# Attention and two feed-forward layers on one core: a third place for raw weights, weight sums at other points of the program, and operand splits in earlier slots

## The chip, the core and the metric

The kernel runs on one core of a Trainium2 chip. A core has five engines that run their own instruction streams side by side: TensorE (PE in the profile, with its weight loads as PEld), VectorE (DVE), ScalarE (ACT), GpSimd (POOL) and SyncE (SP, which here only issues DMA transfers). They wait for each other through semaphores, and each engine executes its stream strictly in order: an instruction that waits holds up everything behind it on its engine. Matrix products go from SBUF through TensorE into PSUM; DMA brings data from HBM into SBUF. The metric is the device time of one execution in microseconds (us), median of several runs.

## The reference

Attention with a soft cap, then a gated layer (SiLU), then a second two-layer network with a parametric ReLU. All of it is float32.

```python
batch, n_heads, seq, head_dim = (2, 12, 448, 64)       # attention
n_tokens, d_model, d_ff = (896, 768, 1536)             # first network; the second has d_ff 2048

scores = scale * np.matmul(q, k.transpose(0, 1, 3, 2))
scores = cap * np.tanh(scores / cap)
attn = np.exp(scores - max); attn = attn / (attn.sum(-1) + 1e-09)
x = attn @ v                                            # heads joined: 896 x 768

xn = x / sqrt(mean(x * x) + 1e-06) * rms_g
g = xn @ w_gate;  x = (silu(g) * (xn @ w_val)) @ w_out

h = x @ w_in;  out = (max(h, 0) + alpha * min(h, 0)) @ w_out2
```

## The kernel before

**Products.** A float32 operand is split into a high part (type fp32r) and a low remainder; a product is high x high + high x low + low x high. ScalarE writes the high part (a cast), VectorE the remainder (original minus high part).

**Weights.** The weights lie in HBM as 68 units of 128 x 768. A unit goes through `w_load` (a DMA of 768 KB issued by SP into a place tagged `raw`, two of them), `w_top` (a cast on ScalarE, L103), `w_bits` (VectorE, L107, which writes the float32 tile `wt` and frees the place), `w_hi` (ScalarE, L120, tile `wh`) and `w_lo` (VectorE, L124, tile `wl`). `w_next(u)`, called right after `w_bits(u)`, issues the load two units further on in `conv_seq`.

**Attention.** 12 pairs of heads with 4 steps each (48 steps). A step holds `qk` (TensorE, scores), `soft` (tanh and exp on ScalarE) and, two steps later, `pv` (TensorE). The list `later` says which other work is written behind which step: `prep` splits the next pair's inputs on VectorE, `evac` copies a pair's result out of PSUM and sends its row sums to a tile `gt` by DMA, `recip` (VectorE) turns these into reciprocals `th`/`tl` and spreads them by two DMAs into `r2` (on GpSimd's queue, the last ones on SP's), `norm` multiplies on TensorE (`rps`, L286) and VectorE (L288, L289), squares on GpSimd (ScalarE for the last four pairs) and adds up `s2` on GpSimd. `rms` (TensorE L309, ScalarE's square root L311, VectorE's reciprocal L312) gives `rstd` of one of the two batches; `xnorm` (L325) applies it.

**The two long layers** ("g", the gate and value weights, and "z", `w_in`) use Strassen's scheme with seven products P1 to P7 per group of two weight blocks (6 groups in g, 4 in z). They need four units (A11, A21, A22, A12) and four sums of them, made on GpSimd (L115): S1 = A21 + A22, S2 = S1 - A11 (written over A11), S3 = A11 - A21 (over A21), S4 = A12 - S2 (over A12). The activations have operands B11, B21, B22, T1 to T4, each with a high and a low tile.

**The two short layers** ("o", `w_out`, and "f", the last `w_out`) read the results of a long layer as moving operands. `ksplit` splits one block of eight rows of them (three casts on ScalarE, L727), `ksplit_low` makes the three remainders on VectorE (L494), in the tiles that the operands T1 to T4 and B11 to B22 leave free. `oslot` computes three outputs at a time, each in a PSUM tile of its own.

**Order.** After the attention the program is a list of 94 slots (one Strassen product of 18 matmuls, or a step of o or f of 36). `do(n, rank, fn, ...)` hangs work on slot n; it is written behind the slot's matmuls, by rank: 0 for `w_hi` (of slot n + 2) and `w_top`, 1 for work on results (`silu`, `times`, `prelu_a` on ScalarE, `prelu_b` and the additions `add21`, `add22`, `u2` on VectorE), 2 for `w_lo` and `ksplit_low`, 3 for `bits`, 4 for the sums, 5 for operands and `ksplit`. g starts at slot 0, o at 38, z at 50, f at 78. PSUM holds four pair tiles in turn: two `s`, two `m`; a product that takes a tile waits until the work on its last content is done.

The functions that the change touches follow.

## Time and profile before

| | us |
|---|---|
| median of 3 runs (644.24 to 651.46) | 648.99 |
| the profiled execution | 650.39 |
| its span from the first to the last instruction | 648.6 |
| TensorE busy (93% of the span) | 602.7 |
| VectorE busy (63%) | 407.8 |
| ScalarE busy (55%) | 354.3 |
| GpSimd busy (19%) | 121.0 |
| time on the chain that ended last: TensorE 66%, VectorE 9%, ScalarE 4%, DMA 4% | |

A row of a timeline or of a wait list names the engine, the line of the kernel, and out<-in by the program's tile names. `L343` are the Strassen products, `L568`, `L570`, `L572` the three kinds of matmul of o and f. TensorE's clock has two levels, 2.4 GHz (a granted clock of 1.00) and 1.2 GHz (0.50); its mean over the span is 0.97.

### The profile page before, as it was taken

How to read it: one execution, taken by the hardware profiler on the slowest of the kernel's cores; microseconds unless marked ns; L12 is line 12 of the kernel's file. 1: busy time of each engine (PE TensorE's matmuls, PEld its weight loads, DVE VectorE, ACT ScalarE, POOL GpSimd, SP SyncE). 2: the span in 40 equal slices, each digit the busy share in tenths (PEclk: the TensorE clock that was granted, in tenths of full speed). 3: DMA queues.
4: the chain of work that ended last, by engine and by line, in shares of the span. 5: the costliest groups of instructions: out<-in, count | busy, mean ns of one | idle time of the engine just before them, and what ended most of it. 6: DMA issues, size and time to landing. Idle time of an engine off the chain costs nothing.

```text
span 648.6 us, 6899 instructions
## 1 busy us (share of the span) xinstructions
PE 602.7 (93%) x2672; PEld 511.0 (79%) x2672; DVE 407.8 (63%) x439; ACT 354.3 (55%) x435; POOL 121.0 (19%) x71
## 2 busy tenths in 40 slices
PE   5999989797999999996999999989789769999997
PEld 4666655475998999995999999979679669999996
DVE  7456679848998966866553565867786567533200
ACT  6999988634734554436444444646566648434101
POOL 0012542253014441310000052301351000000000
PEclk9999999997999999999899999989989969999999
DMA  8556642110033444123224652003321421264002
GB/s 303 197 189 244 231 149 87 28 64 36 0 114 130 146 147 147 49 74 122 99 97 147 199 190 98 0 1 132 112 98 50 146 98 49 98 220 157 1 1 85
DMA packets 18632, 73.47 MB, mean 113 GB/s; under 512 B 5672, under 2 KB 6056, under 8 KB 18600
## 3 DMA queue, kind: packets, MB, share of 16 engines
q1 hardware_dynamic: 15592, 72.82, 32.0%
q0 software_dynamic: 2864, 0.21, 0.4%
q8 instruction: 21, 0.34, 0.2%
q14 instruction: 11, 0.09, 0.0%
q10 hardware_dynamic: 144, 0.00, 0.0%
HBM read 70.14 MB, written 2.75 MB: 112 GB/s over the span
## 4 chain that ended last, share of the span: by engine, by line
PE 66%; DVE 9%; ACT 4%; DMA 4%; issue 2%; POOL 0%; SPq 0%; ACTq 0%; DVEq 0%; POOLq 0%
PE s L343 17%; PE m L343 14%; PE s L570 6%; PE s L572 6%; PE s L568 6%; PE m L570 5%; PE m L572 5%; PE m L568 5%; DMA raw<-w_in 3%; DVE wl L124 1%; DVE b L494 1%; DVE rstd L312 1%; ACT top L103 1%; ACT ks L727 1%; DVE b L794 1%
## 5 line engine op out<-in xcount | busy, mean ns | idle before, releaser
L124 DVE TENSOR_TENSOR wl<-wt,wh 128x768 fp32r<-128x768 f32 x98 | 110.3, 1131 | 89.9 <-ACT wh L120 89.6
L103 ACT CAST top<-raw 128x768 f16<-128x768 bf16 x68 | 73.1, 1076 | 126.2 <-DMA raw<-w_in 125.2
L115 POOL TENSOR_TENSOR wt<-wt 128x768 f32<-128x768 f32 x40 | 89.0, 2229 | 276.9 <-DVE wt L107 198.7
L120 ACT CAST wh<-wt 128x768 fp32r<-128x768 f32 x98 | 80.8, 832 | 68.8 <-PE s L570 15.4
L107 DVE SCALAR_TENSOR_TENSOR wt<-raw,top 128x768 uint32<-128x768 uint32 x68 | 68.3, 1006 | 17.0 <-ACT top L103 12.2
L343 PE MATMUL s<-xh,wh 128*128 128x448 f32 x234 | 62.1, 374 | 2.3 <-DVE b L794 2.3
L343 PE MATMUL s<-xh,wl 128*128 128x448 f32 x234 | 61.5, 371 | 0.0
L343 PE MATMUL s<-xl,wh 128*128 128x448 f32 x234 | 61.4, 370 | 0.0
L343 PE MATMUL m<-xh,wh 128*128 128x448 f32 x186 | 50.9, 380 | 10.2 <-ACT b L447 6.0
L199 PE MATMUL s<-hi 128*128 128x448 f32 x96 | 48.5, 506 | 6.8 <-DVE hi L375 6.5
L568 PE MATMUL s<-ks,wh 128*128 128x448 f32 x176 | 51.0, 371 | 3.9 <-ACT ks L727 3.9
L572 PE MATMUL s<-ks,wl 128*128 128x448 f32 x176 | 50.9, 371 | 0.0
L343 PE MATMUL m<-xh,wl 128*128 128x448 f32 x186 | 49.5, 375 | 1.2 <-DVE wl L124 1.2
L343 PEld LDWEIGHTS s<-xh,wh 128*128 128x128 f32 x234 | 44.2, 190 | 7.8 <-issue 3.2
L343 PE MATMUL m<-xl,wh 128*128 128x448 f32 x186 | 49.2, 373 | 0.0
L343 PEld LDWEIGHTS m<-xh,wh 128*128 128x128 f32 x186 | 35.8, 194 | 15.6 <-ACT b L447 6.4
L343 PEld LDWEIGHTS s<-xh,wl 128*128 128x128 f32 x234 | 44.3, 190 | 4.6 <-DVE wl L124 0.2
L343 PEld LDWEIGHTS s<-xl,wh 128*128 128x128 f32 x234 | 44.4, 190 | 4.4
L568 PE MATMUL m<-ks,wh 128*128 128x448 f32 x160 | 46.6, 373 | 0.5 <-ACT ks L727 0.5
L572 PE MATMUL m<-ks,wl 128*128 128x448 f32 x160 | 46.8, 374 | 0.0
L209 ACT ACTIVATE pt<-s,cinv 128x896 f32<-128x896 f32 (+1 forms) x48 | 43.6, 909 | 5.8 <-PE s L199 4.1
L210 ACT ACTIVATE pt<-pt,cap_t 128x896 f32<-128x896 f32 (+1 forms) x48 | 45.6, 950 | 1.6
(118 smaller groups left out, 987.1 us busy)
## 6 DMA issues: line engine op xcount, KB each, us to landing
raw<-w_in SPq DMA_DIRECT2D x68, 768.0 KB, 4.4
rw<-qk_in SPq DMA_DIRECT2D x11, 928.0 KB, 4.9
vt<-v_in SPq DMA_DIRECT2D x12, 416.0 KB, 5.5
out<-o SPq DMA_DIRECT2D x5, 448.0 KB, 2.5
rw<-qk_in SPq DMA_DIRECT2D x1, 480.0 KB, 4.4
rw<-qk_in SPq DMA_DIRECT2D x1, 448.0 KB, 5.4
out<-o SPq DMA_DIRECT2D x2, 224.0 KB, 2.0
gt<-ea SPq DMA_DIRECT2D x12, 1.8 KB, 1.6
```

Source lines behind the costliest of these rows:

```text
L103: nc.scalar.copy(top_of[u].bitcast(F16)[:, 1::2], raw_t[u].bitcast(BF16)[:, 4:4 * UW + 4:4])
L107: nc.vector.scalar_tensor_tensor(out=f_t[u].bitcast(U32), in0=raw_t.pop(u).bitcast(U32)[:, 1:2 * UW + 1:2], scalar=13, in1=top_of.pop(u), ...
L115: nc.gpsimd.tensor_tensor(out=t, in0=f_t[a], in1=f_t[b], op=op)
L120: nc.scalar.copy(h_t[u], f_t[u].rearrange("p (k m) -> p k m", m=P))
L124: nc.vector.tensor_tensor(out=l_t[u], in0=f_t[u].rearrange("p (k m) -> p k m", m=P), in1=h_t[u], op=ALU.subtract)
L199: nc.tensor.matmul(s[:, n, :S], hi[i][:, S + o:S + o + P], t[hd], start=(m == 0), stop=(m == len(mm) - 1),)
L209: nc.scalar.activation(out=t[:, :n], in_=s[:, :n, :S], func=AF.Tanh, scale=cinv)
L210: nc.scalar.activation(out=t[:, :n], in_=t[:, :n], func=AF.Exp, scale=cap_t)
L343: nc.tensor.matmul(ps[:, r, :S], lhs, rhs, start=first and n == 0, stop=n == len(mm) - 1, skip_group_check=True,)
L568: nc.tensor.matmul(dst[l], wh[:, o, :], xh[l], start=first, stop=False)
L570: nc.tensor.matmul(dst[l], wh[:, o, :], xl[l], start=False, stop=False)
L572: nc.tensor.matmul(dst[l], wl[:, o, :], xh[l], start=False, stop=fin)
```

## The change

Five things are changed; the set of instructions of each engine stays the same.

- `raw` gets three places, and `w_next(u)` loads three units ahead. Behind attention step 2 three loads are issued, not two.
- The sums of g's first two groups: S2 is now made in the attention, one step behind S1; S3 is made as A22 - S2 (the same value), so it comes after S2, and stands at the end of the attention just ahead of S4. In all other groups the order is S1, S2, S3, one slot apart.
- `recip` stands one step earlier (step done + 5), the `norm` of pairs 4 and 5 and all of `rms(0)` one step earlier, the `norm` of pairs 8 and 9 two steps later.
- `rstd` lies in a third of the tile B22h (as `spare`), and the first copied product c11 in the other two thirds; the tile `kx` is given up for a place tagged `ct`.
- `ksplit` of o's blocks 0 and 1 stands at slots o0 - 3 and o0 - 2 (before: o0 - 2, o0), of f's blocks 0 and 1 at f0 - 3 and f0 - 1 (before: f0 - 2, f0); `ksplit_low` follows one slot behind each.

```diff
 G2 = K2N // 4
-WT, WH = 10, 4
+WT, WH, RAW = 10, 4, 3
...
     def w_load(u):
-        raw_t[u] = wpool.tile([P, 4 * UW + 4], U16, tag="raw", name="raw", bufs=2)
+        raw_t[u] = wpool.tile([P, 4 * UW + 4], U16, tag="raw", name="raw", bufs=RAW)
         nc.sync.dma_start(out=raw_t[u][:, 1:4 * UW + 1], in_=w[units[u]].bitcast(U16))
...
     def w_next(u):
-        i = conv_seq.index(u) + 2
+        i = conv_seq.index(u) + RAW
         if i < len(conv_seq):
...
-        w_sum((lay, g, "S3"), (lay, g, "A11"), (lay, g, "A21"), ALU.subtract, home=(lay, g, "A21"))
+        w_sum((lay, g, "S3"), (lay, g, "A22"), (lay, g, "S2"), ALU.subtract, home=(lay, g, "A21"))
...
-    rstd = {}
+    rstd, spare = {}, {}
...
             nc.tensor.matmul(ms[:, :S], ones, t, start=(n == 0), stop=(n == 1))
-        rstd[b] = xpool.tile([P, S], F32, tag="rstd", name="rstd")
+        spare[b] = xpool.tile([P, K3, S], F32, tag="B22h", name="spare")
+        rstd[b] = spare[b][:, 2]
         nc.scalar.activation(out=rstd[b], in_=ms[:, :S], func=AF.Sqrt, scale=1.0 / DM, bias=rms_b)
...
             if j == len(members[n]) - 1 and i < NPAIR - 1:
-                at(done + 6, recip, n)
+                at(done + 5, recip, n)
                 for m, i2 in enumerate(members[n]):
-                    at(done + (10 if n < len(members) - 2 else 8) + m, norm, i2)
+                    at(done + (9 if i == NP - 1 else 10) + m, norm, i2)
             if i == NP - 1:
-                at(done + 13, rms, 0)
+                at(done + 12, rms, 0)
                 for m in range(NP):
-                    at(done + 14 + 2 * m, xnorm, m)
-        for u in conv_seq[:2]:
+                    at(done + 13 + 2 * m, xnorm, m)
+        for u in conv_seq[:RAW]:
             at(2, w_load, u)
...
             at(s0 + 1, w_bits, u)
-            if j < 6:
+            if j < len(conv_seq) - RAW:
                 at(s0 + 1, w_next, u)
...
                 at(s0 + 2, sum1, "g", u[1])
+                at(s0 + 3, sum2, "g", u[1])
         end = NA + LAG
...
             pa[g] = pair_tile(ps_s, "s")
-            sum3("g", g)
-            sum2("g", g)
         recip(len(members) - 1)
...
         rms(B - 1)
-        c11 = [xpool.tile([P, 2, S], F32, tag=f"B22{p}", name="c11") for p in "hl"]
+        c11 = [spare[B - 1][:, :2], xpool.tile([P, 2, S], F32, tag="B22l", name="c11")]
         nc.scalar.copy(c11[0], pa[0][:, :, :S])
...
             w_hi(("g", g, "S2"))
+            sum3("g", g)
+        for g in range(2):
             sum4("g", g)
...
                 do(s1, 4, sum1, lay, g)
-                do(s1, 4, sum3, lay, g)
                 do(max(n1 - 2, s1 + 1), 4, sum2, lay, g)
+                do(max(n1 - 2, s1 + 1) + 1, 4, sum3, lay, g)
                 do(n2 - 1, 4, sum4, lay, g)
...
             do(z0 - 2, 4, sum1, "z", g)
-            do(z0 - 1, 4, sum3, "z", g)
             do(z0 - 1 + g, 4, sum2, "z", g)
+            do(z0 + 1 + g, 4, sum3, "z", g)
             do(z0 + 3 + g, 4, sum4, "z", g)
...
             do(n, 3, bits, u)
-        for u in conv_seq[6:8]:
+        for u in conv_seq[8 - RAW:8]:
             do(0, 6, w_next, u)
...
             def tile_of(tag):
-                if tag == "kx":
-                    return main.tile([P, 2, S], F32R, tag=tag, name="kx")
+                if tag == "ct":
+                    return xpool.tile([P, 2, S], F32R, tag=tag, name="ks", bufs=2)
                 return (xpool if tag[0] == "B" else main).tile([P, K3, S], F32R, tag=tag, name="ks")
...
         o0 = at_of["o", 0, 0]
-        ksplits(o0 - 2, "o", 0, hb, ("T2h", "T2l", "T3h"), 3)
-        ksplits(o0, "o", 1, hb, ("T3l", "B21h", "B21l"), 0)
+        ksplits(o0 - 3, "o", 0, hb, ("T2h", "T2l", "T3h"), 3)
+        ksplits(o0 - 2, "o", 1, hb, ("T3l", "B21h", "B21l"), 0)
         ksplits(o0 + 2, "o", 2, hb, ("T4h", "T4l", "B22h"), 1)
...
         f0 = at_of["f", 0, 0]
-        ksplits(f0 - 2, "f", 0, zt, ("T2h", "T2l", "T1h"), ("B11h", "B11l", "kx"))
-        ksplits(f0, "f", 1, zt, ("T1l", "T3h", "T3l"), 0)
+        ksplits(f0 - 3, "f", 0, zt, ("T2h", "T2l", "T1h"), ("B11h", "B11l", "ct"))
+        ksplits(f0 - 1, "f", 1, zt, ("T1l", "T3h", "T3l"), 0)
         ksplits(f0 + 1, "f", 2, zt, ("B21h", "B21l", "T4h"), 1)
...
             for m in range(3):
-                o = (ct if m % 2 else cu)("o")
+                o = (ct if m == 1 else cu)("o")
                 parts = [slice(0, 2)] if half == 0 or m < 2 else [slice(0, 1), slice(1, 2)]
```

How the engines' streams move at three places:

GpSimd at the end of the attention, before (`s2` is the sum of squares of the second batch; the first four `wt` rows are S3 and S2 of groups 0 and 1, the last two S4):

```order
L300 TENSOR_TENSOR s2_861<-s2_861,sq_977 128x448
L300 TENSOR_TENSOR s2_861<-s2_861,sq_997 128x448
L115 TENSOR_TENSOR wt_399<-wt_237,wt_399 128x768
L115 TENSOR_TENSOR wt_237<-wt_594,wt_237 128x768
L115 TENSOR_TENSOR wt_478<-wt_304,wt_478 128x768
L115 TENSOR_TENSOR wt_304<-wt_668,wt_304 128x768
L300 TENSOR_TENSOR s2_861<-s2_861,sq_1068 128x448
L115 TENSOR_TENSOR wt_742<-wt_742,wt_237 128x768
L115 TENSOR_TENSOR wt_830<-wt_830,wt_304 128x768
```

and in the change:

```order
L300 TENSOR_TENSOR s2_863<-s2_863,sq_997 128x448
L300 TENSOR_TENSOR s2_863<-s2_863,sq_1005 128x448
L300 TENSOR_TENSOR s2_863<-s2_863,sq_1066 128x448
L115 TENSOR_TENSOR wt_401<-wt_578,wt_239 128x768
L115 TENSOR_TENSOR wt_480<-wt_653,wt_314 128x768
L115 TENSOR_TENSOR wt_750<-wt_750,wt_239 128x768
L115 TENSOR_TENSOR wt_832<-wt_832,wt_314 128x768
```

S2 has left for the attention; S3 now stands behind the third addition, next to S4: four sums in a row behind it, where there were two.

ScalarE at the entry of o, before (`top`: `w_top`; `wh`: `w_hi`; `b_2000` rows: `silu` of g's last groups; `ks<-b_1220`, `ks<-b_1600`: `ksplit` of blocks 0 and 1):

```order
L664 ACTIVATE b_2000<-c_1854 128x448
L120 CAST wh<-wt 128x768
L103 CAST top_87<-raw 128x768
L664 ACTIVATE b_2000<-m 128x448
L664 ACTIVATE b_2000<-c_2187 128x448
L727 CAST ks<-b_1220 128x1344 x2
L727 CAST ks<-b_1220 128x896
L120 CAST wh<-wt 128x768
L103 CAST top_86<-raw 128x768
L120 CAST wh<-wt 128x768
L103 CAST top_87<-raw 128x768
L664 ACTIVATE b_2000<-c_2053 128x448
L727 CAST ks<-b_1600 128x1344 x2
```

and in the change:

```order
L666 ACTIVATE b_2000<-c_1855 128x448
L729 CAST ks<-b_1221 128x1344 x2
L729 CAST ks<-b_1221 128x896
L120 CAST wh<-wt 128x768
L103 CAST top_87<-raw 128x768
L666 ACTIVATE b_2000<-m 128x448
L666 ACTIVATE b_2000<-c_2188 128x448
L729 CAST ks<-b_1600 128x1344 x2
L729 CAST ks<-b_1600 128x896
L120 CAST wh<-wt 128x768
L103 CAST top_86<-raw 128x768
L120 CAST wh<-wt 128x768
```

Block 0's casts have moved ahead of one `wh`, one `top` and two `silu`; block 1's stand ahead of two `wh` and two `top` more.

VectorE at the entry of f, before (`b_3486` rows: `prelu_b` and additions of z's last group; `ks<-b_2928`, `kx<-b_2928`: `ksplit_low` of block 0):

```order
L794 SCALAR_TENSOR_TENSOR b_3346<-b_3346,zn 128x896
L124 TENSOR_TENSOR wl<-wt,wh 128x768
L107 SCALAR_TENSOR_TENSOR wt<-raw,top_86 128x768
L794 SCALAR_TENSOR_TENSOR b_3486<-s,b_3486 128x896
L794 SCALAR_TENSOR_TENSOR b_3486<-b_3486,zn 128x896
L494 TENSOR_TENSOR b_3486<-m,b_3486 128x896
L124 TENSOR_TENSOR wl<-wt,wh 128x768
L494 TENSOR_TENSOR ks<-b_2928,ks 128x1344 x2
L494 TENSOR_TENSOR kx<-b_2928,ks 128x896
L107 SCALAR_TENSOR_TENSOR wt<-raw,top_87 128x768
L494 TENSOR_TENSOR b_3486<-m,b_3486 128x896
```

and in the change:

```order
L796 SCALAR_TENSOR_TENSOR b_3347<-b_3347,zn 128x896
L124 TENSOR_TENSOR wl<-wt,wh 128x768
L496 TENSOR_TENSOR ks<-b_2927,ks 128x1344 x2
L496 TENSOR_TENSOR ks<-b_2927,ks 128x896
L107 SCALAR_TENSOR_TENSOR wt<-raw,top_86 128x768
L796 SCALAR_TENSOR_TENSOR b_3487<-s,b_3487 128x896
L796 SCALAR_TENSOR_TENSOR b_3487<-b_3487,zn 128x896
L496 TENSOR_TENSOR b_3487<-m,b_3487 128x896
L124 TENSOR_TENSOR wl<-wt,wh 128x768
L107 SCALAR_TENSOR_TENSOR wt<-raw,top_87 128x768
L496 TENSOR_TENSOR b_3487<-m,b_3487 128x896
```

Block 0's remainders now stand ahead of the two `prelu_b` of z's last group and of its addition `b<-m,b`.

## Rows read from the trace of the kernel before

**Rows 1.** TensorE's waits: line, who released it; us in total, times, longest

```profile
PE m L343 <- ACT b L447: 6.0, 1, 6.0
PE rps L286 <- DMA r<-tl: 5.3, 2, 3.9
PE m L570 <- DVE b L494: 4.6, 1, 4.6
PE s L570 <- DVE ks L494: 4.6, 1, 4.6
...
PE s L568 <- ACT ks L727: 3.9, 1, 3.9
...
PE m L343 <- DVE wl L124: 1.2, 1, 1.2
```

**Rows 2.** Waits of all engines, the longest on ScalarE, in the same columns

```profile
ACT top L103 <- DMA raw<-w_in: 125.2, 31, 8.8
```

**Rows 3.** DMA issues, page part 6: count, KB, us from issue to landing

```profile
raw<-w_in SPq DMA_DIRECT2D x68, 768.0 KB, 4.4
```

**Rows 4.** Three stretches: length, busy us of PE, PEld, DVE, ACT, POOL; granted clock

```profile
305.30:312.20 6.90, 5.13 (x14) 4.57 (x15) 6.90 (x8) 0.91 (x2) 0.00 (x0) 0.51 0.11 24
...
469.20:476.00 6.80, 2.98 (x8) 2.68 (x9) 5.88 (x7) 5.93 (x8) 2.66 (x2) 0.50 0.33 117
...
520.40:530.60 10.20, 5.94 (x16) 5.29 (x17) 8.42 (x8) 3.40 (x5) 0.00 (x0) 0.50 0.15 49
```

**Rows 5.** TensorE's timeline, end of the attention: start, us, instruction [idle before <-releaser]

```profile
133.98 1.11 PE L343 MATMUL s<-xh,wh 128*128 128x448 f32 x3
...
143.24 0.65 PE L286 MATMUL rps<-r,sel_t 128*128 128x448 f32 x2 [1.45 <-DMA r<-tl]
...
155.73 0.74 PE L343 MATMUL m<-xh,wh 128*128 128x448 f32 x1 [2.92 <-ACT xh L513]
```

**Rows 6.** VectorE's timeline, 79 to 153 us

```profile
79.55 0.18 DVE L272 TENSOR_TENSOR tl<-gt,th 64x28 fp32r<-64x28 f32 x1
...
137.75 1.54 DVE L271 CAST th<-gt 64x28 fp32r<-64x28 f32 x1
139.32 1.78 DVE L272 TENSOR_TENSOR tl<-gt,th 64x28 fp32r<-64x28 f32 x1
...
149.79 2.95 DVE L312 RECIPROCAL rstd<-rstd 128x448 f32<-128x448 f32 x1 [2.02 <-ACT rstd L311]
```

**Rows 7.** GpSimd's timeline, end of the attention

```profile
135.48 7.47 POOL L115 TENSOR_TENSOR wt<-wt 128x768 f32<-128x768 f32 x4
```

**Rows 8.** ScalarE's timeline, entry of o

```profile
293.76 1.07 ACT L103 CAST top<-raw 128x768 f16<-128x768 bf16 x1 [6.39 <-DMA raw<-w_in]
294.70 0.57 ACT L664 ACTIVATE b<-c 128x448 f32<-128x448 f32 x1
```

**Rows 9.** VectorE's timeline, entry of o

```profile
305.47 4.02 DVE L494 TENSOR_TENSOR b<-b,ks 128x1344 fp32r<-128x1344 f32 x3
```

**Rows 10.** ScalarE's timeline in z, group 2

```profile
465.30 1.07 ACT L103 CAST top<-raw 128x768 f16<-128x768 bf16 x1 [5.39 <-DMA raw<-w_in]
...
469.06 1.05 ACT L103 CAST top<-raw 128x768 f16<-128x768 bf16 x1
...
472.08 0.88 ACT L447 COPY b<-m 128x896 f32<-128x896 f32 x1
```

**Rows 11.** VectorE's timeline in z, group 2

```profile
459.78 0.94 DVE L107 SCALAR_TENSOR_TENSOR wt<-raw,top 128x768 uint32<-128x768 uint32 x1
```

**Rows 12.** ScalarE's timeline, entry of f

```profile
507.98 1.08 ACT L103 CAST top<-raw 128x768 f16<-128x768 bf16 x1 [6.39 <-DMA raw<-w_in]
...
509.89 1.23 ACT L791 ACTIVATE zn<-zn,al_t 128x448 f32<-128x448 f32 x2
...
518.06 3.35 ACT L727 CAST ks<-b 128x1344 fp32r<-128x1344 f32 x3
```

**Rows 13.** TensorE's timeline, from z to f

```profile
519.41 0.68 PE L568 MATMUL s<-ks,wh 128*128 128x448 f32 x2 [3.88 <-ACT ks L727]
```

## The prediction

> **What bounds the kernel now.** I read the page's shares first: TensorE is busy for 602.7 of 648.6 us, so time can be won only where TensorE stands still or runs slow. The list of waits says where: a few single stalls, of 1.4 to 6.0 us, not a steady shortage [rows 1]. Then I asked for the busy time and clock of the stretches behind the longest stalls. In each of them the granted clock is at the lower of its two levels (0.50 and 0.51 of 2.4 GHz): TensorE had stood idle and then took up work, and 5.13, 2.98 and 5.94 us of busy time went by at half speed [rows 4]. So a stall costs its own length and about half of the slow busy time behind it: 2.6, 1.5 and 3.0 us at these three places. Last I followed each stall back on the engine that released it. At the entries of o and f TensorE wants the split operands, and ScalarE, which has to cast them first, stood for 6.39 us before a `top` that waits for a raw transfer [rows 8, 12]. In z's group 2 it wants a PSUM tile that ScalarE copies out late (L447), after 5.39 us before such a `top` [rows 10]. ScalarE waits 125.2 us for raw weights in 31 waits, most of them harmless [rows 2]: with two places the load of unit u + 2 can't be issued before VectorE's `bits` of unit u, and lands 4.4 us later [rows 3].
>
> **The change part by part.**
>
> *Third raw place.* It adds no instruction and no bytes; loads move earlier by one unit. The 4.4 us of a transfer then lie behind one more unit's work. The third load at attention step 2 is one more transfer among the first inputs; for it I take 0 (at most its own 4.4 us, if it held up an input that TensorE wants) [rows 3].
>
> *z, group 2.* The first of the two `top` in question no longer waits (-5.39), and the copy could end at 472.96 - 5.39 = 467.6, against TensorE's arrival at about 473.0 - 6.0 = 467.0 [rows 1, 10]. But the `top` behind it is tied to its own load, which is now issued after the `bits` that ended at 460.72, and lands at 460.72 + 4.4 = 465.1 [rows 3, 11]. From the start of that `top` to the copy's end 3.9 us passed (its cast was at 469.06, 3.0 before the copy's start at 472.08) [rows 10]: 465.1 + 3.9 = 469.0. So I leave a wait of 2.0 of the 6.0, hence -4.0, plus a part of the clock's 1.5 (I take 0.2): **-4.2**. Bounds: 0, if VectorE's `bits` are late too, and -7.5 (6.0 + 1.5).
>
> *Entry of o.* Block 0's casts now stand behind the first `silu` that follows the waiting `top`. Even if no load came sooner, they would start at 294.70 + 0.57 = 295.3, with one more `top` and two `silu` no longer ahead of them, and end at 298.6 (the same three casts of block 0 of f take 3.35); the three remainders take 4.02 [rows 8, 9, 12]. TensorE wanted the first remainder 4.6 us before it got it, which was about 1.5 us after VectorE began at 305.47, so at about 302.4 [rows 1, 9]. VectorE has from 298.6 to then for a third of 4.02. The stall goes whether or not the loads come sooner: -4.6 - 2.6 = **-7.2**. Bounds: -3 (an addition that frees the third PSUM tile is now queued behind the remainders) and the -7.2 itself, which is all there is.
>
> *Entry of f.* Casts: before, they stood behind a `top` with 6.39 us of waiting and six activations of the last results; now they stand ahead of four of the latter. Without an earlier load they would start behind the activations of 509.89, at 511.1 instead of 518.06, and end at 514.5; with 6 us of the `top`'s wait gone, near 508.5 [rows 12]. TensorE arrives at 519.41 - 3.88 = 515.5 [rows 13]: both stalls, 3.9 and 4.6, go, and 3.0 of the clock [rows 1, 4]. What is late next: the remainders (4.02) now stand on VectorE ahead of two `prelu_b` and an addition, which free the second and third PSUM tile of f. By my count, with a `wl` and a `bits` ahead of them, the remainders end near 514.6, and the last of the three behind them near 518.8. The third tile is wanted after 12 matmuls of 36; the 36 that ran from 133.98 to 143.24 - 1.45 = 141.8 took 7.8, so 12 take at most 2.6, to 517.9 to 518.1 [rows 5, 13]. I put the new wait at 0.9. Sum: -3.9 - 4.6 - 3.0 + 0.9 = **-10.6**. Bounds: -11.5 (no new wait) and -3.6 (no earlier load: the chain 4 us later, so a new wait of 4.9, and the half clock again).
>
> *End of the attention.* Three moves with opposite signs. (1) `norm` of pairs 8 and 9 goes two steps later, behind the last `pv`. TensorE's longest wait for `r2`, 3.9 us, stood ahead of the first of these; it goes, as that matmul now comes when the reciprocals have long landed [rows 1]. The last steps hang on ScalarE's exponentials as well, so of the 3.9 I take 3: the first Strassen product starts at 131 instead of 133.98 [rows 5]. (2) The four sums that stood ahead of the last `recip` are gone from there (7.47 us in one piece). Beside them `th` and `tl` took 1.54 and 1.78 us, where `tl` takes 0.18 elsewhere [rows 6, 7]; without them 2.9 us are saved, on top of the 3 of the earlier start, and the second `rps` comes at about 138.4 instead of 143.24, its 1.45 of waiting gone [rows 5]. (3) But four sums in a row now follow the third addition of squares, where two stood. Four took 7.47 [rows 7], and in their new place they last until VectorE is through the reciprocal of `rstd` (2.95) and in the `wl` and the `xnorm` behind it [rows 6], which make T1, for which TensorE already waits 2.9 us [rows 5]. I charge 2 us for that. So T1 comes at 155.73 - 4.85 + 2 = 152.9: **-2.8**. Earlier in the attention, `recip` and two `norm` move one step earlier: TensorE may wait there for a row sum or an `r2` that lands no sooner than before, and GpSimd's squaring behind it gets two more sums ahead of it (2 x 1.87, a quarter of 7.47 each) [rows 7]. I take it that the rest of the attention, where ScalarE sets the pace, swallows this. Bounds for the whole: -5 and +2.
>
> A rule of the Trainium skill speaks against move (3) and the spreading of the sums: page "SBUF — State Buffer", section "Who interferes with whom", has VectorE and GpSimd share a port pair under an exclusive lock, so that a VectorE instruction with two SBUF inputs and a GpSimd instruction that reads SBUF shut each other out. The rows of `th` and `tl` agree with it. By that rule alone every sum costs VectorE up to its own length wherever VectorE has no gap, and the time would be that of the last rival below.
>
> *At nothing:* the tiles `spare` and `ct` add no wait that I could find, since their former contents are read a slot or more before; if one did, I would price it by the wait for a tile that is copied out late, 6.0 at most [rows 1].
>
> **Sum.** -2.8 - 7.2 - 4.2 - 10.6 = -24.8. The profiled execution took 650.39 us, so 625.6; it lies 1.4 us above the median of 648.99, so **624 us**.
>
> **Rivals.**
>
> *The waits move rather than vanish.* Each engine works in order, and what steps back (four activations, two `prelu_b`, additions, `wh`) is wanted too. For it: z's residual and f's new wait above are of this kind. Against: at o and f the operands are ready with 2 us or more in hand. If half of every term comes back: 650.4 - 12.4 - 1.4 = 636.6.
>
> *All of it is won.* z's copy in time (-7.5), the attention's end at its bound (-5), f without a new wait (-11.5), o with 7.2: 650.4 - 31.2 - 1.4 = 617.8. Against it is the load behind the 460.72 `bits`.
>
> *The loads don't come sooner,* because VectorE's `bits`, not the second place, is late: z gives 0, f -3.6, o -3, the attention +2 with the sums in a row: 650.4 - 4.6 - 1.4 = 644.4.
>
> *Slower: the sums hit VectorE.* S3 now follows S2 in each group, so three slots of each group hold a sum instead of two, and GpSimd's sums stand beside `wl` more often. One wait of TensorE for a `wl` is in the trace, 1.2 us [rows 1]; with slow matmuls behind it, as behind the stall of z (1.5 of 6.8 us) [rows 4], a hit costs some 2.7 us. If the ten groups of g and z have one each, and two more fall into the attention (12 x 2.7 = 32.4), they outweigh o, z and f (22.0): 650.4 - 22.0 + 32.4 - 1.4 = 659.4. It decides from eight hits on (21.6), and beyond 1% from ten or eleven. Against it: VectorE is 63% busy, and most of the forty sums of before delayed nobody.
>
> **How the numbers follow.** Forecast (620 to 632) 0.58; waits that move (632 to 641) 0.19; all won (614 to 620) 0.11; loads not sooner (641 to 648) 0.07; slower 0.05. A measurement of this kernel can tell about 1% (6.5 us) from no change. Below 642.5 lie the first three, 0.88; within 1% most of the fourth, 0.07; above 655.5 the last, 0.05. The likeliest case alone has 620 to 632. The range runs from 614 to 638: it leaves out the upper part of the second case (0.04) and the last two, 0.16 in all.
>
> **What would show it.** In the profile after, TensorE should have no wait for `ks` or remainders at the entries of o and f and no half-clock stretch there; any wait there should name `prelu_b` or an addition. The wait for the copy L447 should be 2 us or less. ScalarE's waits for `raw` should fall far below 125 us. The waits of `rps` on `r2` should shrink, and T1's wait (L513) should grow past 2.9. If these hold and the time does not, new waits on `wl` or `wh` behind the moved sums are where I was wrong.

## The result and the profile after

The changed kernel takes 620.81 us (median of 4 runs, 616.82 to 623.11), the kernel before 647.13 (4 runs): a ratio of 0.958, 95% interval 0.950 to 0.966. Four more runs on another occasion gave 0.960 (0.955 to 0.965). The forecast was 624 us with a range of 614 to 638. The profiled execution of the changed kernel spans 615.0 us (616.8 in all), that of the kernel before 648.6.

TensorE's waits in the changed kernel, in the columns of [rows 1]:

```profile
PE m L344 <- ACT xh L515: 6.1, 3, 4.6
PE rps L286 <- DMA r<-tl: 2.8, 3, 1.5
PE s L344 <- DVE b L796: 2.3, 1, 2.3
PE s L570 <- DVE b L796: 1.1, 1, 1.1
...
PE m L570 <- DVE b L496: 0.5, 1, 0.5
PE m L344 <- ACT b L449: 0.2, 1, 0.2
```

The stalls at the entries of o and f for split operands (4.6, 3.9, 4.6) are gone; 1.1 and 0.5 us for a `prelu_b` and an addition have come at f. The waits of `rps` for `r2` have shrunk from 5.3 us (longest 3.9) to 2.8 (longest 1.5). The wait for the late copy in z's group 2 has gone from 6.0 to 0.2 us, the wait for T1 (`xh`) has grown from a longest of 2.9 to 4.6. ScalarE's list has hardly any raw transfer left, 5.3 us against 125.2 [rows 2]:

```profile
ACT top L103 <- DVE wt L107: 37.9, 12, 6.0
ACT top L103 <- DMA raw<-w_in: 5.3, 4, 2.6
```

The first of these lines is new. A `top` is written into one of two fixed tiles, and VectorE's `bits` (L107) free them; with three places for `raw` these two tiles are the next limit. None of TensorE's waits above ends on a `top` or a `bits`.

The stretches that answer to those of [rows 4] (length; busy us of PE, PEld, DVE, ACT, POOL; granted clock; DMA share; GB/s), with the end of the attention ahead of them:

```profile
153.00:161.00 8.00, 6.48 (x16) 5.04 (x17) 7.80 (x13) 1.81 (x4) 0.00 (x0) 0.52 0.01 2
295.00:303.00 8.00, 8.00 (x42) 7.41 (x41) 8.00 (x9) 3.11 (x4) 0.00 (x0) 1.00 0.27 98
450.00:457.00 7.00, 6.76 (x34) 5.83 (x32) 6.49 (x6) 5.17 (x8) 3.08 (x3) 1.00 0.63 219
491.00:502.00 11.00, 9.36 (x46) 7.99 (x45) 11.00 (x12) 10.70 (x13) 0.00 (x0) 1.00 0.43 144
```

At the entry of o, in z's group 2 and at the entry of f the clock stays at 1.00. Behind the wait for T1 it is at 0.52.

Both kernels issue the same 2672 matmuls on TensorE, and behind the attention they stand in nearly the same order, so the two traces can be laid beside each other by the matmul's number. The start of matmul number n, changed less before:

| n | place | difference, us |
|---|---|---|
| 600 | behind the T1 products | -2.4 |
| 1150, 1200 | before and behind the entry of o | -4.7, -12.7 |
| 1850, 1950 | before and behind z's late copy | -14.6, -23.3 |
| 2050, 2150 | before and behind the entry of f | -23.7, -33.4 |
| 2650 | end | -33.6 |

The steps at the places make 8.1, 8.7 and 9.7 us. Between the places the difference grows slowly by nearly 5 us; that is not the change (last section).

To compare the experiments, each stretch gets an **extra time**: the time from its first to its last matmul, less 0.2027 us for each matmul, which is what one takes where nothing waits at a granted clock of 1.00 (the shorter of two spacings, last section). It holds the waits and the slow clock behind them. The stretches are matmuls 1151 to 1235 (o), 1852 to 1950 (z) and 2095 to 2156 (f).

| kernel | o | z group 2 | f |
|---|---|---|---|
| before | 8.2 | 9.4 | 11.7 |
| changed | 0.0 | 0.7 | 2.2 |
| two raw places | 6.5 | 10.7 | 7.5 |
| old split slots | 1.5 | 0.7 | 7.0 |
| third place only | 1.4 | 1.1 | 7.0 |
| splits only | 5.2 | 11.0 | 7.8 |

### The profile page after: what moved, and what is told of

The parts are those of the page before. It is cut to its first block, busy times and chain, and to the rows that moved or that the text cites. A ratio compares the mean times of both kernels' runs of the same rounds, so it can differ in the third digit from the quotient of the medians.

```text
span 615.0 us, 6896 instructions
## 1 busy us (share of the span) xinstructions
PE 589.1 (96%) x2672; PEld 506.4 (82%) x2672; DVE 403.5 (66%) x439; ACT 355.7 (58%) x435; POOL 120.0 (20%) x71
## 4 chain that ended last, share of the span: by engine, by line
PE 83%; DVE 7%; DMA 4%; issue 3%; ACT 2%; POOL 0%; SPq 0%; ACTq 0%; DVEq 0%; POOLq 0%
PE s L344 19%; PE m L344 16%; PE s L574 6%; PE s L572 6%; PE s L570 6%; PE s L199 5%; PE m L570 5%; PE m L572 5%; PE m L574 5%; PE ob L229 4%; PE oa L225 4%; DVE b L496 1%; DMA r<-tl 1%; DMA gt<-eb 1%; DVE b L796 1%
## 5 line engine op out<-in xcount | busy, mean ns | idle before, releaser
L124 DVE TENSOR_TENSOR wl<-wt,wh 128x768 fp32r<-128x768 f32 x98 | 107.7, 1105 | 91.0 <-ACT wh L120 89.7
L120 ACT CAST wh<-wt 128x768 fp32r<-128x768 f32 x98 | 81.1, 833 | 94.6 <-PE s L572 23.3
L107 DVE SCALAR_TENSOR_TENSOR wt<-raw,top 128x768 uint32<-128x768 uint32 x68 | 67.7, 999 | 7.8 <-ACT top L103 7.3
L199 PE MATMUL s<-hi 128*128 128x448 f32 x96 | 49.0, 510 | 7.4 <-DVE hi L376 6.6
L574 PE MATMUL m<-ks,wl 128*128 128x448 f32 x160 | 45.4, 365 | 0.0
```

Of the source, the lines that this page charges most:

```text
L107: nc.vector.scalar_tensor_tensor(out=f_t[u].bitcast(U32), in0=raw_t.pop(u).bitcast(U32)[:, 1:2 * UW + 1:2], scalar=13, in1=top_of.pop(u), ...
L120: nc.scalar.copy(h_t[u], f_t[u].rearrange("p (k m) -> p k m", m=P))
L124: nc.vector.tensor_tensor(out=l_t[u], in0=f_t[u].rearrange("p (k m) -> p k m", m=P), in1=h_t[u], op=ALU.subtract)
L199: nc.tensor.matmul(s[:, n, :S], hi[i][:, S + o:S + o + P], t[hd], start=(m == 0), stop=(m == len(mm) - 1),)
L574: nc.tensor.matmul(dst[l], wl[:, o, :], xh[l], start=False, stop=fin)
```

## The experiments: taking one part back

**The changed kernel again.**

> The changed kernel once more, unchanged, as the reference for the three beside it: about 0.958 of the kernel before. In the two profiles read so far 50 matmuls took 10.33 us in long stretches of the kernel before and 10.13 us in the changed one, with a granted clock of 1.00 in both, which adds up to some 5 us. If that belongs to the change, a profile here shows 10.13 again; if it belongs to the execution, it may show either.

Measured: 622.26 us, ratio 0.960 (0.955 to 0.965); the extra times are within 0.3 us of those of the first profile. The spacing is 0.203 us again through most of its length.

**Two raw places.**

```diff
-WT, WH, RAW = 10, 4, 3
+WT, WH, RAW = 10, 4, 2
```

> The changed kernel with two places for raw weights again, all else as changed. Theory (each place of the program has its own cause): the wait for the late copy in z's group 2 comes back, 6.0 + 1.5 of slow clock + 1.2 of the wait for a remainder, so +8.5; the entries of o and f stay free, since their casts stand far enough ahead, apart from a wait of up to 4.9 at f for the third PSUM tile. Together +8.5 to +14, about 0.972 to 0.98 of the kernel before. Rival (the third place does everything): nearly the whole gain goes, +24. Rival (the earlier splits do everything): under +3.

Measured: 640.70 us, 0.991 (0.989 to 0.993), which is 18.4 us above the changed kernel measured beside it: more than the 8.5 to 14 of the theory, less than the 24 of the rival. The waits of TensorE show why:

```profile
PE m L344 <- ACT b L449: 6.2, 1, 6.2
...
PE s L570 <- DVE b L796: 3.1, 1, 3.1
...
PE m L570 <- DVE b L496: 2.8, 1, 2.8
...
PE s L572 <- DVE ks L496: 1.8, 1, 1.8
PE m L344 <- DVE wl L124: 1.5, 1, 1.5
```

z's wait is back (6.2, and 1.5 for a `wl` ahead of it), as forecast. At f TensorE waits 1.8 for a remainder and 3.1 for a `prelu_b`. And o is not free: there the earlier splits have only exchanged one stall for another. ScalarE and then VectorE at the entry of o in this kernel:

```profile
292.11 1.08 ACT L103 CAST top<-raw 128x768 f16<-128x768 bf16 x1 [6.58 <-DMA raw<-w_in]
293.06 0.57 ACT L666 ACTIVATE b<-c 128x448 f32<-128x448 f32 x1
293.53 3.36 ACT L729 CAST ks<-b 128x1344 fp32r<-128x1344 f32 x3
296.79 0.83 ACT L120 CAST wh<-wt 128x768 fp32r<-128x768 f32 x1
```

```profile
297.65 0.96 DVE L124 TENSOR_TENSOR wl<-wt,wh 128x768 fp32r<-128x768 f32 x1 [3.37 <-ACT wh L120]
298.53 4.02 DVE L496 TENSOR_TENSOR b<-b,ks 128x1344 fp32r<-128x1344 f32 x3
302.47 0.95 DVE L107 SCALAR_TENSOR_TENSOR wt<-raw,top 128x768 uint32<-128x768 uint32 x1
303.34 0.62 DVE L496 TENSOR_TENSOR b<-m,b 128x448 f32<-128x448 f32 x1
```

The casts stand right behind the late `top` and its `silu`, as the forecast said. But the `wh` cast is queued behind them, so VectorE waits 3.37 us for it before a `wl`, and only then come the remainders and behind them the addition that reads a PSUM tile which the block of o needs. TensorE goes on at 304.01, after 2.8 us. The raw transfer is late in both orders, and in each of them something that TensorE needs stands behind it.

**Old split slots.**

```diff
-ksplits(o0 - 3, "o", 0, ...)
-ksplits(o0 - 2, "o", 1, ...)
+ksplits(o0 - 2, "o", 0, ...)
+ksplits(o0, "o", 1, ...)
...
-ksplits(f0 - 3, "f", 0, ...)
-ksplits(f0 - 1, "f", 1, ...)
+ksplits(f0 - 2, "f", 0, ...)
+ksplits(f0, "f", 1, ...)
```

> The changed kernel with the operand splits of o's and f's blocks 0 and 1 in the slots of the kernel before; three raw places stay. Theory: with loads in time the casts come sooner than before, but not soon enough: o waits about 2 us for its first remainder instead of 4.6, f about 2.5 for its casts and 4 for its remainders, and half of each stretch behind runs at the slow clock: +10 to +13, about 0.975 of the kernel before. Rival (the third place does everything): within 2 us of the changed kernel. Rival (splits alone): +17 as in the forecast's sum for o and f.

Measured: 624.66 us, 0.965 (0.961 to 0.969), 2.4 us above the changed kernel, with intervals that overlap. By place it is 1.5 at o and 4.8 at f. TensorE's waits:

```profile
PE s L572 <- DVE ks L496: 4.4, 1, 4.4
...
PE m L572 <- DVE b L496: 0.9, 1, 0.9
```

With loads in time f's casts come in time even from the old slots; one wait for the remainders stays. The earlier slots are worth about 6 us by place, while the medians differ by 2.4 only; both are far from the 17.8 that the forecast put down to them.

**End of the attention as before.**

```diff
+            w_sum(("g", g, "S3"), ("g", g, "A11"), ("g", g, "A21"), ALU.subtract, home=("g", g, "A21"))
+            sum2("g", g)
         recip(len(members) - 1)
...
             w_hi(("g", g, "S2"))
-            sum3("g", g)
-        for g in range(2):
             sum4("g", g)
```

(and the old steps of `recip`, `norm` and `rms`; the S2 sums in the attention, `sum2` at step s0 + 3, are left out).

> The changed kernel with the end of the attention as before: sums S2 and S3 of the first two groups ahead of the last reciprocals, reciprocals, norm and rms in their old steps. Theory: +2 to +3 (T1 comes at 155.7 instead of 153.0, and TensorE runs at the slow clock after the wait for r2 again). Rival (the sums' new places gain more, by freeing VectorE in the attention): over +5. Rival (four sums in a row cost as much as the rest gains): under +1.

Measured: 619.95 us, 0.958 (0.953 to 0.963). That is no loss against the changed kernel (0.960); a gain of 2 us and no gain can't be told apart here, since executions of one kernel differ by 5 us. The trace tells more: T1's first matmul is at 155.33 here and at 153.19 in the changed kernel measured beside it, but the changed kernel then runs longer at the slow clock, having stood idle for 4.6 us and not 2.9. At matmul 600 the changed kernel is some 2 us ahead. This profile has the 1.8 us back at z's start, where no slow clock followed (last section). The theory's 2 to 3 us were about right for the place, and they are too small to be seen in the time.

**One part alone.** The third place alone has the old split slots and the attention of before, that is the second and third diff of this section together; the splits alone have two places and the attention of before, the first and the third.

> Of the three parts only the third raw place (with the tiles that make room for it): operand splits and the end of the attention as before. Revised theory (the third place carries most of the gain also at the entries of o and f, because ScalarE no longer stands before a transfer; the other parts overlap with it): the late copy in z no longer counts, o waits about 1 us and f about 4.4 for remainders, 0.966 of the kernel before, 625 us. Theory of the forecast (z 8.5 by the third place, o and f 17.8 by the splits): 0.983 to 0.987, 637 to 639 us.

Measured: 623.78 us, 0.967 (0.960 to 0.974).

> Of the three parts only the earlier operand splits: two raw places, the end of the attention as before. Revised theory: o and f exchange their old stalls for new ones behind late additions and prelu (about 3 us each) and z keeps its 6 us: 0.99 of the kernel before, 641 us. Theory of the forecast: 0.975 or less, 631 us.

Measured: 642.39 us, 0.992 (0.990 to 0.994).

Both came out as the revised theory had them. The two are nearly additive: by place the third raw place alone takes off 6.8 + 8.3 + 4.7 = 19.8 us, the splits alone 3.0 - 1.6 + 3.9 = 5.3, both together (in the changed kernel) 8.2 + 8.7 + 9.5 = 26.4. All these kernels keep the moved tiles and the new order of the sums in the later groups. With two places z costs 10.7 and 11.0 with them, against 9.4 before, so they don't bring the gain there.

## The experiments: the waits that are left

**The sums in another gap.**

```diff
                 at(done + 5, recip, n)
+                if n == len(members) - 2:
+                    for g in range(2):
+                        at(done + 5, sum3, "g", g)
...
             w_hi(("g", g, "S2"))
-            sum3("g", g)
-        for g in range(2):
             sum4("g", g)
```

> The changed kernel with the two S3 sums of groups 0 and 1 moved forward on GpSimd, behind the last-but-one spread of reciprocals, where GpSimd (127.2 to 132.2) and VectorE (127.4 to 130.2) are both idle; behind the third addition of squares two sums remain instead of four. Theory (GpSimd's sums shut out VectorE's two-operand work): the first application of rstd falls from 2.23 to 0.7 us, the remainder ahead of it from 1.20 to 0.9, the wait for T1 from 4.57 to about 2.7, and the kernel gains 2 us (less than the 5 us by which its executions differ, so the trace has to show it). Rival (the chain to T1 hangs on the reciprocal of 2.95 us, not on the sums): the wait stays at 4.5.

First the changed kernel, VectorE ahead of T1 and GpSimd beside it:

```profile
148.28 1.20 DVE L124 TENSOR_TENSOR wl<-wt,wh 128x768 fp32r<-128x768 f32 x1
149.41 2.23 DVE L326 SCALAR_TENSOR_TENSOR xf<-xf,g_t,spare 128x448 f32<-128x448 f32 x1
```

```profile
142.52 8.64 POOL L115 TENSOR_TENSOR wt<-wt 128x768 f32<-128x768 f32 x4
```

Then this kernel, with VectorE at both places and GpSimd:

```profile
127.76 4.48 DVE L332 TENSOR_TENSOR xl<-xf,xh 128x448 fp32r<-128x448 f32 x1
...
150.35 0.89 DVE L124 TENSOR_TENSOR wl<-wt,wh 128x768 fp32r<-128x768 f32 x1
151.16 0.67 DVE L326 SCALAR_TENSOR_TENSOR xf<-xf,g_t,spare 128x448 f32<-128x448 f32 x1
```

```profile
128.17 3.58 POOL L115 TENSOR_TENSOR wt<-wt 128x768 f32<-128x768 f32 x2
```

Half of the expectation held. With two sums less behind the third addition, the first application of `rstd` takes 0.67 instead of 2.23 us and the `wl` 0.89 instead of 1.20, and the wait for T1 is 2.9. But the gap was not empty: an `xl` of the first batch (0.63 us elsewhere) met the two sums and took 4.48 us, which delayed all that follows, so that T1 starts at 153.41, no sooner than in the changed kernel. The price of the sums was mostly moved, not saved. The time was 616.34 us, 0.953 (0.949 to 0.957). By place under 1 us of that is explained (the multiplied reciprocals come 2 us later, the wait and the slow clock behind it cost 2.5 us less); the rest is no more than executions differ by. This is the rule that the forecast took from the Trainium skill ("SBUF — State Buffer", "Who interferes with whom"), and the trace agrees: an instruction of VectorE with two SBUF inputs waits for GpSimd's sum, here for two of them in succession.

**f's split one slot earlier still.**

```diff
-ksplits(f0 - 3, "f", 0, ...)
+ksplits(f0 - 4, "f", 0, ...)
```

> The changed kernel with the split of f's block 0 one more slot earlier, so that its remainders stand ahead of one more bits, prelu and weight remainder on VectorE. Theory (f's two remaining waits, 1.1 and 0.5 us, are for a prelu and an addition queued behind the remainders): they go, -1.6 and a little of the slow clock. Rival (those waits hang on ScalarE's side of the prelu): they stay.

Measured: 618.13 us, 0.956 (0.951 to 0.961), f's extra time 2.4 against 2.2: nothing gained. The wait of 1.1 for the `prelu_b` went, that of 0.5 for the addition grew to 1.6. VectorE there:

```profile
491.88 1.09 DVE L796 SCALAR_TENSOR_TENSOR b<-s,b 128x896 f32<-128x896 f32 x1 [0.45 <-ACT b L793]
493.99 1.09 DVE L796 SCALAR_TENSOR_TENSOR b<-b,zn 128x896 f32<-128x896 f32 x1 [1.01 <-ACT zn L793]
495.00 1.08 DVE L496 TENSOR_TENSOR b<-m,b 128x896 f32<-128x896 f32 x1
```

VectorE is now ahead of ScalarE, and the addition that frees the tile stands behind a `prelu_b` that frees none and waits for ScalarE. So theory and rival were both right, each for one of the two waits.

**No idle time ahead of T1.** 22 matmuls of no use on operands that are at hand, ahead of the first product with T1; their results are overwritten.

```diff
+        for n in range(warm):
+            nc.tensor.matmul(ps[:, 0, :S], wh[:, n % K3, :], oper["B21"][0][:, n % K3, :], start=True, stop=True, ...)
```

> The changed kernel with 22 matmuls of no use (at 0.203 us, 4.5 us in all, their results overwritten) in TensorE's wait for T1, ahead of the first product that reads T1. It measures what the slow clock costs there. Theory (an idle TensorE comes back at the lower clock): the granted clock stays at or near 1.00 behind the wait, and the stretch of 80 matmuls from the last product of the attention on, 27.2 us with 6.6 us of waits, loses up to 4.4 us; the waits of 0.5 and 1.0 us for the second and third tile of T1 stay. The kernel gains 3 to 4 us. Rival (the clock there falls for another reason than the idle time): no gain, or 0.5 us lost.

The same stretches in the changed kernel and then in this one (columns as above):

```profile
148.00:153.00 5.00, 0.43 (x4) 0.04 (x2) 4.93 (x6) 2.93 (x4) 3.15 (x2) 0.74 0.00 0
153.00:156.00 3.00, 1.48 (x3) 0.57 (x3) 2.87 (x6) 1.13 (x2) 0.00 (x0) 0.50 0.02 5
156.00:160.00 4.00, 4.00 (x11) 3.57 (x12) 3.96 (x6) 0.37 (x1) 0.00 (x0) 0.50 0.00 0
```

```profile
148.00:153.00 5.00, 4.92 (x24) 4.13 (x23) 4.93 (x6) 2.94 (x4) 3.16 (x2) 1.00 0.00 0
153.00:156.00 3.00, 0.94 (x3) 0.38 (x3) 2.87 (x6) 1.13 (x2) 0.00 (x0) 0.88 0.02 5
156.00:162.00 6.00, 6.00 (x16) 5.36 (x17) 5.91 (x9) 1.13 (x2) 0.00 (x0) 0.50 0.00 0
```

The clock stays at 1.00 through the wait, and then falls behind the next waits (0.7 and 1.3 us, for T1's second and third tile). The slow stretch has moved from 153 to 160 us to 156 to 162. Nothing is gained at this place; the expected 3 to 4 us were wrong. The time, 618.45 us, 0.954 (0.949 to 0.959), differs by less than the executions do.

**All of it together.** The two S3 sums stand on GpSimd behind a small addition that reads the last `tl`, the first T1 product goes tile by tile of T1, f's split is one slot earlier and the last `prelu` of quarter 3 one slot later.

```diff
-        recip(len(members) - 1)
+        tl = recip(len(members) - 1)
+        nc.gpsimd.tensor_tensor(out=scr, in0=tl.bitcast(F32), in1=tl.bitcast(F32), op=ALU.add)
+        for g in range(2):
+            sum3("g", g)
...
+            mm = [(a, xh, k, r) for k in range(K3) for a in (wh, wl) for r in range(2)]
...
-            prelu(max(at_["P7"], at_["P5"]) + 2, g, 3, c22)
+            prelu(max(at_["P7"], at_["P5"]) + 2 + (g == G2 - 1), g, 3, c22)
```

> Three edits at the two places where the changed kernel still waits. (1) The two S3 sums of groups 0 and 1 on GpSimd behind a small addition that reads the last reciprocals' tl, so that they run while VectorE waits for the multiplied reciprocals; two sums instead of four stay behind the third addition. (2) The first product with T1 goes by tile of T1 in its outer loop. (3) The split of f's block 0 one slot earlier and the last group's prelu of quarter 3 one slot later, so that the addition that frees f's third PSUM tile comes sooner. Theory: xl of the first batch stays at 0.63 us (4.48 in the kernel with the sums in the gap), the first application of rstd takes 0.67, the wait for T1 falls from 4.57 to 2.9 and f's waits of 1.1 and 0.5 us go; with (2) 1 us more: -4 us against the changed kernel, 0.954 of the kernel before. Rival (the sums collide with something else, or the addition hangs on ScalarE): the waits move and the time stays.

Measured: 616.52 us, 0.950 (0.944 to 0.957). GpSimd:

```profile
136.44 0.23 POOL L469 TENSOR_TENSOR scr<-tl 64x28 f32<-64x28 f32 x1 [1.02 <-DVE tl L272]
136.63 3.62 POOL L115 TENSOR_TENSOR wt<-wt 128x768 f32<-128x768 f32 x2
```

The sums run while VectorE has nothing to do; `xl` is back at 0.63, the application of `rstd` takes 0.67, T1's first matmul comes at 151.6 and the second T1 product starts at 157.4 instead of 161.4. f's extra time is 0.6. Another 1.8 us come at z's start, where no slow clock follows in this profile (last section); no edit aimed at that.

> The kernel with the S3 sums behind the last reciprocals, the first T1 product by tiles of T1 and the earlier split at f, once more, in five rounds, beside the next one: 0.950 of the kernel before. Its profile shows whether the matmul spacing of 0.207 us, which it had in most of its length in the first profile, belongs to the kernel (0.207 again) or to the execution (0.203 in other stretches).

Measured: 613.81 us, 0.947 (0.943 to 0.951). The profile has the short spacing almost throughout, so the spacing belongs to the execution.

**The same with 13 matmuls of no use** in the wait that is left (2.9 us).

> The same, with 13 matmuls of no use (2.6 us) in the wait for T1, which is 2.9 us there and has only 0.2 us of waiting behind it. In the changed kernel such matmuls only moved the slow clock behind the next wait of 1.3 us. Theory (the slow clock follows idle time): with no such wait left, the granted clock stays at 1.00 from 148 to 165 us and the second T1 product starts 1.5 to 2 us sooner after the first matmul of the first; about 0.947 of the kernel before. Rival (the clock falls there anyway): no gain.

Measured: 610.26 us, 0.945 (0.941 to 0.949), the fastest kernel here, faster than both kernels that were compared. The granted clock:

```profile
148.00:152.00 4.00, 3.76 (x19) 3.09 (x18) 3.93 (x7) 2.86 (x5) 0.00 (x0) 1.00 0.01 2
152.00:156.00 4.00, 3.29 (x16) 2.48 (x15) 3.87 (x7) 1.11 (x2) 0.00 (x0) 1.00 0.01 2
```

It stays at 1.00 up to 165 us. But from the first T1 matmul to the second product it is 4.9 us (151.61 to 156.52) against 5.8 (151.60 to 157.40) and 5.05 (151.10 to 156.15) in the two profiles without them: at full clock TensorE arrives sooner at T1's third tile and waits for it, 0.7 us. So the forecast 1.5 to 2 us were not there, but 0.1 to 0.9; whether the kernel without these matmuls is really slower, the overlapping intervals don't settle.

## Why the prediction was right, and where it was not

The time was right: 624 forecast, 621 measured. By its steps:

- **Stall plus half of the slow time behind it.** This held at o: 4.6 + 0.5 of waits and 2.6 of clock make 7.7, and the extra time was 8.2. It held at f: 3.9 + 4.6 + 3.0 = 11.5, and 11.7 was there.
- **Entry of o, -7.2.** Measured -8.2 by place. Its reasoning failed in one point: "the stall goes whether or not the loads come sooner". With two places o keeps 6.5 of 8.2. What was overlooked is the `wh` behind the casts on ScalarE, for which VectorE waits ahead of the remainders. The bound of -3 names the addition behind the remainders, which is what TensorE waits for there; with two places o gained 1.7 us (8.2 - 6.5), and 3.0 with the old end of the attention.
- **Entry of f, -10.6.** Measured -9.5. The new wait came where it was foreseen, behind `prelu_b` and an addition (1.1 and 0.5 against 0.9). Without earlier loads the forecast had -3.6, and with two places it is 11.7 - 7.5 = 4.2.
- **z, group 2, -4.2.** Mis-sized: -8.7 by place. The forecast left a wait of 2.0 because the second `top` hangs on its own load, issued after the `bits` that ended at 460.72. The mechanism is there: in the changed kernel that `bits` ends at 442.67, and the `top` starts 4.5 us later, the time of a transfer, after waiting for it:

```profile
441.72 0.95 DVE L107 SCALAR_TENSOR_TENSOR wt<-raw,top 128x768 uint32<-128x768 uint32 x1
```

```profile
447.20 1.08 ACT L103 CAST top<-raw 128x768 f16<-128x768 bf16 x1 [0.63 <-DMA raw<-w_in]
...
450.27 0.88 ACT L449 COPY b<-m 128x896 f32<-128x896 f32 x1
```

  But the forecast kept that `bits` where it was in the trace of before. It starts 18.1 us sooner (441.72 against 459.78), where TensorE is some 14.7 us ahead of its old times: VectorE itself, no longer behind late `top`s, runs 3.4 us further ahead. The wait shrinks to 0.2, and the 1.2 for a `wl` and the slow clock go too.
- **End of the attention, -2.8.** The places came out almost to the tenth: first Strassen product 131 forecast and 130.99 measured, the last `rps` 138.4 and 138.91, T1 152.9 and 152.99. (The 138.4 doesn't follow from the rows, which give 131 + 7.8 = 138.8.) The sums do block VectorE there: without them `th` and `tl` take 0.17 and 0.18 us, not 1.54 and 1.78. Only `tl` has the two SBUF inputs of the rule that the forecast cites; `th`, a cast with one input, slowed as well, which the rule as cited there doesn't cover. T1's longer wait brought a longer slow stretch, so 2 us are left, and no run shows them in the time.
- **What was put at nothing.** That the places agree is luck in part. The forecast let the rest of the attention swallow the earlier steps and the two S2 sums, and it didn't. The matmuls of the scores (L199) stand in the same order in both kernels. At 85.1 us of the kernel before, one of them starts 3.0 us later in the changed kernel (2.3 in its second profile), and at 118.6 us still 2.5 (2.6) later; with the end of the attention as before it is 0.2 us earlier at both. A `norm` moved one step earlier waits for `r2`, and the split of the next pair's inputs (`hi`, two SBUF inputs) meets the first S2 sum. First the row of before, then those of the changed kernel:

```profile
80.80 1.16 DVE L176 TENSOR_TENSOR hi<-rw,hi 64x960 fp32r<-64x960 f32 x1
```

```profile
80.13 3.59 DVE L176 TENSOR_TENSOR hi<-rw,hi 64x960 fp32r<-64x960 f32 x1
...
80.88 1.82 POOL L115 TENSOR_TENSOR wt<-wt 128x768 f32<-128x768 f32 x1
...
82.77 0.44 PE L286 MATMUL rps<-r,sel_t 128*128 128x448 f32 x1 [1.49 <-DMA r<-tl]
```

  This `hi` takes 3.59 us in all ten profiles with the new attention and 1.16 in all four with the old. The last matmul of the scores then starts 1.9 us earlier than before: so some 4.4 are won around the wait for `r2` (3.9 us), of which the forecast took 3. So the 131 comes of a loss put at nothing and a gain put too low.
- **Which part pays.** This was wrong. The forecast gave the third place 4.2 us and the splits 17.8. Alone, the third place brings some 20 us by place and the splits 5. At o and f the late casts were themselves late because of raw transfers, and the forecast had the 6.39 us in its rows; it credited the removal to the edit that it looked at first.
- **Sum.** By place 8.2 + 8.7 + 9.5 + 2.4 (at matmul 600) = 28.8 against 24.8. The terms missed by 1.0, 4.5, 1.1 and 0.4 us, and only f's and the attention's were put too high. The profiles differ by 33.6; some 5 us of that is the spacing, which was long in the profiled execution of the kernel before. The medians differ by 26.3 and 25.1.
- **Rivals.** The waits did move in part where a part of the change stood alone (o and f with two places), not in the whole. The slower case did not come: no new wait for a `wl`, and the old one is gone. "All of it is won" came true at o and at z, not at f and in the attention. The sums cost where they met VectorE: on the way to T1 and in the attention.

## What to carry to other kernels

Where an engine works in order and waits for transfers, price a deeper buffer by all work that is queued behind those waits, and let the work that issues the next transfer move too; a fixed time from the old trace is only a bound. Two edits that attack one stall should be priced alone and together, since moving the consumer may only exchange the stall for the next one in the queue. Work on GpSimd that is off the path still has a price for what VectorE does beside it, so it wants a gap that is empty in the trace, and if need be a small dependency that holds it until then.

## What the runs showed of the hardware

**Two spacings at one granted clock.** In long stretches matmuls of the same form follow each other at 0.207 or at 0.203 us, with a granted clock of 1.00. Here is the same kernel (the sums behind the last reciprocals) in two executions, at the same time of the program; three matmuls to a row:

```profile
200.64 0.78 PE L357 MATMUL s<-xh,wh 128*128 128x448 f32 x3
201.26 0.78 PE L357 MATMUL s<-xh,wl 128*128 128x448 f32 x3
```

```profile
199.73 0.77 PE L357 MATMUL s<-xh,wh 128*128 128x448 f32 x3
200.34 0.77 PE L357 MATMUL s<-xh,wl 128*128 128x448 f32 x3
```

In the 14 profiles the spacing holds over long stretches. It changes mostly where TensorE waits, if only briefly, but in five of them it goes from 0.207 to 0.203 near matmul 1700 with no wait there. The first of these two executions has 0.207 for some 1760 matmuls after the attention, the second for some 120: at 0.004 us each, 6.6 of the 7.1 us by which the profiled executions differ (616.7 and 609.6). The kernel before had it for some 1500 (6 us), the changed one for some 200. The runs of one kernel spread over 3 to 9 us here, so a part of the change worth 2 us can't be seen in four or five runs, only in the trace. That the spacing makes most of this spread is shown for this one pair only, and what sets it stays open.

**The slow clock after a short wait comes or not.** The wait of 2.3 us at z's start (L796) is in all profiles. In some a stretch at the slow clock follows and the place costs 4.1 to 4.4 us of extra time, in others none follows and it costs 2.5 to 2.9: six profiles and eight. The granted clock of the 6 us behind the wait is 0.72 in the six and 1.00 in the eight. The two kernels with two profiles each show the same in both, so whether it belongs to the kernel or to the execution stays open.
